# A recurrent attention kernel with a feed-forward layer: weight transfers moved to GpSimd's queue, w_out prepared in one operation, decay loads in pairs

## The chip, the cores and the metric

The kernel runs on one core of a Trainium2 chip. Its engines are TensorE (PE, matrix products), VectorE (DVE), ScalarE (ACT), GpSimd (POOL) and SyncE (SP, which here issues transfers). Each engine takes its own instructions in order and waits on semaphores for the others. The metric is the time of one execution in microseconds on the device, lower being better; a profiled execution also gives a span, from its first to its last instruction.

## The reference

The first part is a linear-attention recurrence over 768 steps for 4 batches and 8 heads of width 48. The state decays by a given factor `w` for every step and channel. The second part takes the 3072 rows of 384 numbers that come out and applies a layer of width 1024, with a softmax gate and a normalization between its two weight matrices.

```python
for t in range(S):
    kt, vt, rt, wt = (k[:, :, t], v[:, :, t], r[:, :, t], w[:, :, t])
    cur = np.einsum('bhd,bhe->bhde', u[None] * kt, vt)
    y[:, :, t] = np.einsum('bhd,bhde->bhe', rt, state + cur)
    state = wt[:, :, :, None] * state + np.einsum('bhd,bhe->bhde', kt, vt)
...
h = x @ w_in
e = np.exp(h - h_max)
sm = e / (np.sum(e, axis=-1, keepdims=True) + 1e-09)
solu = h * sm
ln = (solu - mu) / np.sqrt(var + 1e-06) * g_ln
return (ln @ w_out).astype(np.float32)
```

All inputs and the output are float32.

## The kernel before

The work is cut into 24 units, one for each of 6 chunks of 128 steps and each of the 4 batches; the batch runs fastest, so units 4 to 7 are the second chunk of batches 0 to 3. Within a chunk the recurrence becomes matrix products. For one unit the steps, with the names by which the list of the order calls them, are these:

- `ldw`, `ldk`, `ldr`, `ldv` load four tiles of 128 x 8 x 48 numbers through SP, each row of 48 numbers (192 bytes) being one piece of the transfer.
- `lw` takes the logarithm of w (ACT), `cum` sums it over time by matmuls with triangular matrices, `exp` exponentiates the sums in place (ACT), `et` and `kp` scale (DVE).
- `p`, `q`, `dg`, `dv` form the bonus with u, `qa` being a shorter way to the sum in `dg`; `vb` casts v to bfloat16.
- `kt` and `kr` transpose and copy, `M`, `m`, `sel` make the masked scores, `Y` and `y` the attention's output (with an x behind it, `Y` adds the bonus by one more matmul), `S` and `st` the new state, `X` and `xT` its transpose.
- `H` multiplies by w_in (24 matmuls), `e` exponentiates (ACT), `he` multiplies (DVE), `hq` squares, `Oa` and `Ob` multiply by the prepared w_out (`w2`) and gather sums; `sq`, `qm`, `lv`, `rs` compute the scale of a row; `o` applies it and `sto` stores.

A long text, `ORDER`, writes out the order of all these steps. Each word is a step, a unit and, where there is a choice, the engine (`a` ACT, `v` DVE, `g` POOL). The class `InOrder` ties every instruction of an engine behind the one before it on that engine, so this text is each engine's program; on the profile nearly all instructions carry the line of that class (L71). The words `dm` are matmuls on zeros whose results are not used.

Set-up that stands in the same order: `ldwin` loads w_in in three pieces of 512 KB and `ldwout` loads w_out in two of 768 KB, all through SP, as float32. `win` casts each piece of w_in to bfloat16 (ACT). `gw` scales a slice of w_out, 128 x 384, by the gain (eight slices, on ACT, POOL and DVE), `mean` multiplies all eight by a constant matrix on TensorE, `mean_sb` copies the mean, and `wt` adds it to each slice (eight additions, all on POOL), which gives `w2`. `small` loads u and the gain, `rows` and `ubc` spread them over the partitions. The constants of `make_identity` are not tied into POOL's order by `InOrder`, and stand behind `p` of unit 0 on POOL.

Of the kernel before, what the change touches and what calls it, by code (L numbers as in the profile page):

```python
# [9 lines left out]
F32 = mybir.dt.float32  # L10
# [4 lines left out]
SQUARE = mybir.ActivationFunctionType.Square  # L15
IDENTITY = mybir.ActivationFunctionType.Identity
# [8 lines left out]
dm5 dm3 dm18 dm1 ldw0 ldr0 small dm16 dm8 ldk0 lw0 ldw1 ldr1 cum0 exp0 et0 lw1 rows cum1 ldk1 p0g ldw2 kp0 exp1 ubc kt0 p1g kr0v ldr2 M0 ldk2 ldv0 et1  # L25
kp1 lw2 m0a q0g kt1 kr1v ldwin2 cum2 q1g sel0 dg0 exp2 M1 dm10 et2 vb0a kp2 m1a ldwin1 ldv1 kt2 win2a dg1 dv0g kr2v win1a vb1a Y0 y0v sel1 ldwin0 M2
win0a dm6 X0 m2v dv1v ldwout0 dm4 p2g Y1 q2g S1 y1v ldwout1 qa2 gw1a gw0a dm2 X1 xT0v xT1v dg2 H0 H1 ldw3 e0 st1 S0 dm13 ldv2 gw4v gw6v gw3g he0 ldk3
gw5a dm12 dm17 ldw4 st0 gw7a ldr3 e1 ldk4 lw3 gw2g mean mean_sb:a vb2g ldw5 dv2g he1 Y2 ldr4 cum3 wt2g y2v exp3 lw4 et3 p3v hq0a wt3g cum4 wt1g X2 dm0
wt0g ldk5 dm9 ldr5 exp4 lw5 ldw6 wt4g kp3 S2 kt3 ldv3 cum5 st2 ldw7 wt7g ldv4 et4 kr3a xT2v wt6g ldr6 Oa0 kp4 p4v exp5 wt5g M3 q3v et5 m3a kt4 kr4v
ldk6 Oa1 kp5 hq1a H2 M4 q4g kt5 Ob0 ldv5 sel3 ldw8 lw6 vb3a e2 dg3 kr5a dv3g m4v sq0a dg4 vb4g dv4g p5g vb5g Ob1 ldr7 M5 lw7 ldk7 Y3x ldv6 he2 m5v qm0  # L30
q5g p6g y3a cum6 X3 xT3v sq1v Y4 qm1 exp6 y4v H3 lv0 lv1 et6 ldr8 X4 hq2v ldk8 kp6 Oa2 dg5 o0a xT4a dv5g p7g sto0 ldw9 S4 e3 S3 st4 st3 q6g H4 Y5 vb6g
q7g ldr9 o1a he3 kt6 lw8 S5 Ob2 e4 ldk9 y5v cum7 ldr10 he4 kr6a st5 X5 hq3a sq2a exp7 M6 Oa4 ldv7 ldk10 ldr11 Oa3 qm2 m6v cum8 ldv8 qa6 et7 xT5a sto1
dg6 ldr12 ldk11 lv2 kp7 qa7 Ob3 dv6g exp8 p8g ldw10 p9v kt7 et8 o2a dg7 sq3g kp8 H5 qm3 q8g hq4a lv3 ldv9 e5 ldw11 Y6x kr7v ldv10 p10g M7 vb7g o3v Ob4
ldw12 kt8 m7v y6a q10g lw9 X6 sq4v he5 cum9 xT6a qm4 ldk12 exp9 kr8a dg8 et9 dv7g Y7 hq5g H6 e6 sto2 kp9 Oa5 ldw13 kt9 y7v lv4 X7 dg10 q9g Ob5 kr9a
he6 vb8g ldv11 ldk13 dv8g ldr13 sq5a o4a M8 ldw14 hq6g m8v S7 M9 qm5 vb10g xT7a p11g ldv12 m9v lv5 Oa6 H7 dg9 st7 lw10 Y8 o5a e7 cum10 vb9g ldw15
exp10 Ob6 y8v he7 sq6g X8 sto3 et10 dv9g S6 kp10 ldk14 xT8a lw12 S8 q11g H8 lw11 lw13 cum11 st8 e8 dv10g st6 Oa7 qm6 kt10 Y9x p12g exp11 hq7v kr10a
lv6 Ob7 y9a he8 M10 et11 S9 ldw16 sto4 o6a ldr14 X9 xT9a kp11 cum12 qa11 Oa8 ldr15 exp12 hq8g m10v p13g ldv13 vb11g ldk15 st9 H9 sq7v et12 qm7 kt11
q12g ldv14 lw14 ldr16 kp12 ldk16 lv7 e9 Y10x q13g sto5 y10a o7v ldk17 kr11v he9 cum13 exp13 ldv15 et13 dg11 kt12 kp13 Ob8 X10 sto6 M11 kr12a sq8g Oa9
qa12 ldk18 dv11g ldr17 dg13 M12 m12v kt13 ldw17 vb12g xT10a qm8 S10 m11a sel11 H10 kr13v M13 lw15 st10 ldv16 hq9a Y11x lv8 p15g e10 y11a m13v vb13g
sto7 o8a Ob9 dg12 p14g ldr18 ldv17 sq9v dv12g p16g X11 ldw18 cum14 xT11a S11 he10 Y12 H11 exp14 S12 qm9 st11 y12v lv9 et14 kp14 q14g dv13g st12 hq10g  # L40
o9a ldv18 e11 Y13 X12 cum15 xT12a ldr19 he11 exp15 kt14 Oa10 y13v sto8 hq11g kr14a vb15a q15g lw16 S13 H12 vb14g et15 ldk19 kp15 e12 dg14 X13 M14 p17g
dv14g kt15 ldw19 m14v xT13a he12 kr15a Ob10 H13 q17g sto9 hq12g sq10a st13 M15 Y14 m15v ldv19 qm10 lv10 vb16g Oa11 e13 lw18 q16g S14 lw17 o10v y14v
cum16 he13 ldw20 exp16 dg15 et16 hq13v Ob11 dv15g X14 kp16 Oa12 p18g sq11a p19g xT14a st14 qm11 lv11 H14 Ob12 o11a e14 cum17 q19g kt16 sq12v ldk20 Y15
sto10 he14 exp17 q18g qm12 Oa13 sto11 kr16a et17 hq14g y15v cum18 kp17 lv12 Ob13 M16 ldr20 ldk21 o12v exp18 dg17 X15 vb17g sq13v kt17 m16a et18 qm13
Oa14 xT15v kp18 kr17v sel16 lv13 H15 o13a lw19 dg16 e15 kt18 M17 dv17g dv16g vb19g ldv20 kr18v m17a lw20 Ob14 Y16 he15 M18 y16v sq14v S16 qm14 dg18
cum19 X16 ldv21 hq15g xT16v m18a exp19 Oa15 H16 ldw21 sel17 S15 dg19 lv14 o14a et19 kp19 Y17 lw21 ldr21 st16 e16 cum20 sel18 vb18g st15 y17v exp20
Ob15 sto12 ldk22 ldr22 X17 sto13 kt19 sq15v ldv22 xT17a he16 dv18g Y18 qm15 kr19a dv19g kp20 p20v y18v hq16g H17 M19 Oa16 lv15 X18 q20g Ob16 m19v o15a
e17 xT18a ldw22 lw22 p22g cum21 sq16v he17 qm16 p21g dg20 ldw23 hq17g ldv23 exp21 Y19 kt20 H18 vb20g ldr23 Oa17 lv16 y19v kp21 q21g kr20v o16a cum22
e18 he18 dv20g kt21 exp22 Ob17 kr21a M20 X19 sq17g S17 qm17 m20a lv17 kp22 qa21 sel20 lw23 S18 xT19v sto14 o17a st17 hq18g M21 Oa18 ldk23 m21v kt22
cum23 H19 sto15 st18 exp23 kr22v vb21a kp23 dg21 dv21g sto16 Y20 Y21 vb22a M22 q22g S19 e19 m22a vb23g y20v X20 p23v st19 he19 q23g Ob18 kt23 xT20a  # L50
sq18v H20 qm18 kr23a sel22 M23 y21v lv18 o18a X21 dg22 hq19v xT21v Oa19 m23a dv22v dg23 sel23 Y22 Ob19 y22v e20 he20 H21 dv23g Y23 sto17 X22 sq19a
Oa20 y23v X23 qm19 lv19 hq20g o19a xT22v e21 xT23v H22 e22 he21 Ob20 sto18 hq21g sq20a qm20 lv20 H23 he22 Oa21 Oa22 sto19 Ob21 e23 hq22g sq21a o20v
qm21 lv21 Ob22 he23 hq23v Oa23 sto20 sq22v sq23a qm22 o21v Ob23 sto21 lv22 qm23 Oc23 o22v sto22 lv23 dm14 oz23v dm15 o23a stz23 dm7 sto23 dm11 dm19
# [25 lines left out]
def kernel(  # L79
# [38 lines left out]
    def load(name, src):  # L118
        def stage(i):
            c, b = units[i]  # L120
            L = live[i]
            if name in "kr":

                if "k_and_r" not in L:
                    L["k_and_r"] = io.tile([C, 2, H, 64], F32, tag="kr_in", name="kr_in")
                t = L["k_and_r"][:, "kr".index(name)]
            else:
                t = io.tile([C, H, 64], F32, tag=name + "_in", name=name + "_in")
            L[name] = t[:, :, :D]
            sp.dma_start(out=L[name], in_=src[b, :, c * C:(c + 1) * C, :].rearrange("h t d -> t h d"))  # L130
        return stage
# [4 lines left out]
    win_f = consts.tile([128, KM, DF], F32)  # L136
    win_v = moe_w_in.rearrange("(ko ki) f -> ki ko f", ki=128)
    wout_f = consts.tile([128, KF, DM], F32)
# [5 lines left out]

    def load_w_in(j):
        sp.dma_start(out=win_f[:, j, :], in_=win_v[:, j, :])

    def load_w_out(half):
        part = slice(half * KF // 2, (half + 1) * KF // 2)
        sp.dma_start(out=wout_f[:, part, :], in_=wout_v[:, part, :])  # L150
# [3 lines left out]
    nc.gpsimd.memset(uti_neg, -1.0)  # L154
    nc.gpsimd.affine_select(out=uti_neg, in_=uti_neg, compare_op=ALU.is_ge, fill=0.0, base=0,
                            pattern=[[1, C]], channel_multiplier=-1)
    uts = consts.tile([C, C], BF16)
    nc.gpsimd.memset(uts, 1.0)
    nc.gpsimd.affine_select(out=uts, in_=uts, compare_op=ALU.is_gt, fill=0.0, base=0,
                            pattern=[[1, C]], channel_multiplier=-1)  # L160
    ident = consts.tile([C, C], BF16)
    make_identity(nc, ident)
# [12 lines left out]
    lw_t = [consts.tile([C, H, 64], BF16, name=f"lw{j}") for j in range(NR)]  # L175
    kp_t = [consts.tile([C, 2, H, 64], BF16, name=f"kp{j}") for j in range(NR)]
    for j in range(NR):
        nc.vector.memset(lw_t[j][:, :, D:], 0.0)
        nc.vector.memset(kp_t[j][:, :, :, D:], 0.0)
# [4 lines left out]
    win_sb = consts.tile([128, KM, DF], BF16)  # L184
    w2 = consts.tile([128, KF, DM + 1], BF16)

    mean_w = consts.tile([128, 128], BF16)
    nc.vector.memset(mean_w, -1.0 / DF)
    nc.vector.memset(w2[:, :, DM:], 1.0 / RDF)

    ident_f = consts.tile([KF, KF], F32)
    make_identity(nc, ident_f)
# [4 lines left out]
    gw = consts.tile([128, KF, DM], BF16)  # L197
# [12 lines left out]

    def copy(engine, out, in_):
        if engine is act:
            act.copy(out=out, in_=in_)
        else:
            engine.tensor_copy(out=out, in_=in_)
# [6 lines left out]
    def setup_w_in(j, engine):  # L222
        copy(engine, win_sb[:, j, :], win_f[:, j, :])


    def setup_gain(f, engine):
        if engine is act:
            act.activation(out=gw[:, f, :], in_=wout_f[:, f, :], func=COPY, scale=gr[:, f:f + 1])
        else:
            engine.tensor_scalar(out=gw[:, f, :], in0=wout_f[:, f, :], scalar1=gr[:, f:f + 1], scalar2=None, op0=MULT)  # L230

    def setup_mean():
        m_ps = small.tile([128, DM], F32, tag="s", name="mean_ps")
        for f in range(KF):
            pe.matmul(m_ps, lhsT=mean_w, rhs=gw[:, f, :], start=(f == 0), stop=(f == KF - 1))
        live[0]["mean_ps"] = m_ps

    def setup_mean_copy(engine):
        copy(engine, mean_sb, live[0]["mean_ps"])
# [400 lines left out]
```

The softmax here doesn't subtract the row's maximum and nothing guards it: scores larger than these inputs give would overflow.

## Time and profile before

| | |
|---|---|
| three runs | 157.39, 151.35 and 157.56 us, median 157.39 |
| profiled execution | 151.29 us, of which 149.6 us are its span |
| mean granted TensorE clock | 0.966 |
| busy: TensorE, DVE, ACT, POOL | 137.2, 127.0, 119.7, 122.9 us |
| transfers | 27.09 MB in 104970 packets, of which 100329 are under 512 bytes |

Busy time is the sum of an engine's instructions. A group of instructions is named by engine, operation and tiles, with a count and the mean length of one. The costliest groups are the matmuls of `O` (42.3 us for 200), those of `H` (35.9 us for 576), DVE's `he` (29.2 us for 24, 1.218 each), POOL's squares `hq` (26.5 us for 14, 1.892 each), ACT's `e` (24.5 us for 24, 1.020 each) and DVE's `kp` (22.8 us for 24, 0.948 each). Matmul lengths overlap one another, so a group's sum can exceed the time it took up. An SP row's length contains the wait for room in the transfer queue.

### The profile page before, as it was taken

The page shows a single profiled execution, that of the slowest core. Times are in us where ns is not written, and L with a number is a line of the kernel's source. Part 1 is how long each engine was busy: PE and PEld are TensorE (multiplying, and loading weights), DVE is VectorE, ACT ScalarE, POOL GpSimd, SP SyncE. Part 2 cuts the span into 40 slices and gives each one's busy share as a digit, 9 for nine tenths or more (in the row PEclk, how much of TensorE's full clock was granted, in tenths as well). Part 3 has the DMA queues.
Part 4 walks back from the last instruction along what each step waited for, and adds up shares of the span by engine and source line. Part 5 has one row for each costly group of instructions (what it writes and reads, how often), then busy time and mean ns, then how long its engine had stood idle before and what let it go on. Part 6 is the DMA issues. An engine that isn't in the chain of part 4 may idle for free.

```text
span 149.6 us, 5293 instructions
## 1 busy us (share of the span) xinstructions
PE 137.2 (92%) x2154; PEld 108.7 (73%) x2156; DVE 127.0 (85%) x231; ACT 119.7 (80%) x232; POOL 122.9 (82%) x152
## 2 busy tenths in 40 slices
PE   5676887698999999999999999999999999999993
PEld 2254584576886887887878888878787878888780
DVE  7547849999999798999989989988999999997661
ACT  3466768989798979799898998898998798895651
POOL 3366965999989799999989999999798989975900
PEclk9965599999999999999999999999999999999999
DMA  4999998999989999979999999999989211011113
GB/s 95 199 211 314 385 318 169 221 196 184 201 160 234 183 225 204 240 151 228 207 200 219 240 210 235 202 249 188 254 194 228 62 57 53 7 53 57 48 48 119
DMA packets 104970, 27.09 MB, mean 181 GB/s; under 512 B 100329, under 2 KB 104562, under 8 KB 104946
## 3 DMA queue, kind: packets, MB, share of 16 engines
q1 hardware_dynamic: 104946, 26.75, 79.2%
q8 instruction: 17, 0.28, 0.8%
q14 instruction: 7, 0.06, 0.1%
HBM read 22.03 MB, written 4.72 MB: 179 GB/s over the span
## 4 chain that ended last, share of the span: by engine, by line
PE 57%; POOL 10%; DMA 10%; DVE 8%; SPq 8%; ACT 3%; issue 3%; POOLq 0%; DVEq 0%
PE o_ps L71 20%; PE h_ps L71 16%; SPq L71 7%; DMA wout_f<-in_moe_w_out_dram 6%; POOL w L71 5%; PE kr_ps L71 4%; PE y_ps L71 4%; PE s_ps L71 3%; PE cum_ps L71 3%; PE m_ps L71 3%; DMA kr_in<-in_k_dram 3%; PE x_ps L71 2%; POOL dv L71 2%; DVE kp L71 1%; DVE he L71 1%
## 5 line engine op out<-in xcount | busy, mean ns | idle before, releaser
L71 PE MATMUL o_ps<-w,he 128*128 128x385 bf16 (+2 forms) x200 | 42.3, 315 | 0.3 <-ACT sq L71 0.3
L71 PE MATMUL h_ps<-xT,win_sb 128*128 128x128 bf16 x576 | 35.9, 219 | 0.1
L71 PEld LDWEIGHTS <-win_sb 128*128 128x128 bf16 x576 | 32.9, 98 | 0.8 <-issue 0.2
L71 DVE TENSOR_TENSOR he<-h_ps,e 128x1024 bf16<-128x1024 f32 x24 | 29.2, 1218 | 2.9 <-ACT e L71 2.8
L71 PE MATMUL o_ps<-inv_col,e 128*128 128x1 bf16 x192 | 31.1, 165 | 0.0
L71 ACT ACTIVATE e<-h_ps 128x1024 bf16<-128x1024 f32 x24 | 24.5, 1020 | 6.2 <-PE h_ps L71 6.1
L71 POOL TENSOR_TENSOR hq<-he 128x1024 bf16<-128x1024 bf16 x14 | 26.5, 1892 | 2.6 <-DVE he L71 2.1
L71 PEld LDWEIGHTS <-he 128*128 128x128 bf16 x208 | 19.7, 96 | 10.5 <-issue 0.3
L71 ACT ACTIVATE cum_ps<-cum_ps 128x772 f32<-128x772 f32 (+1 forms) x24 | 19.3, 803 | 5.3 <-PE cum_ps L71 4.1
L71 DVE TENSOR_TENSOR kp<-cum_ps,kr_in 128x768 bf16<-128x768 f32 x24 | 22.8, 948 | 0.2 <-ACT cum_ps L71 0.2
L71 POOL TENSOR_TENSOR q<-p,u_bc 128x384 bf16<-128x384 bf16 x23 | 21.2, 925 | 0.7 <-DVE p L71 0.5
L71 POOL TENSOR_TENSOR dv<-vb,dg 128x384 bf16<-128x384 bf16 x22 | 18.5, 845 | 3.0 <-ACT vb L71 1.1
L71 PEld LDWEIGHTS <-kp 128*128 128x128 bf16 x272 | 17.3, 100 | 4.4 <-DVE kp L71 2.3
L71 POOL TENSOR_TENSOR p<-kr_in 128x384 bf16<-128x384 f32 x18 | 18.4, 1025 | 2.5 <-DMA kr_in<-in_k_dram 2.4
L71 DVE TENSOR_TENSOR m<-m_ps,uts 128x1024 bf16<-128x1024 f32 x14 | 17.0, 1222 | 3.0 <-PE m_ps L71 2.9
L71 PEld LDWEIGHTS <-e 128*128 128x128 bf16 x192 | 18.3, 96 | 0.1
L71 PE MATMUL kr_ps<-ident,kp 128*128 128x128 bf16 x192 | 15.7, 228 | 1.9 <-DVE kp L71 1.9
L71 PEld LDWEIGHTS <-kr 64*128 64x128 bf16 (+1 forms) x272 | 10.7, 98 | 4.9 <-DVE kr L71 2.1
L71 ACT COPY kr<-kr_ps 128x1024 bf16<-128x1024 bf16 x13 | 13.2, 1015 | 0.6 <-PE kr_ps L71 0.6
L71 ACT ACTIVATE lw<-w_in 128x384 bf16<-128x384 f32 x23 | 11.7, 523 | 2.1 <-DMA w_in<-in_w_dram 2.1
L71 PE MATMUL m_ps<-kr 64*128 64x128 bf16 x192 | 10.2, 229 | 2.2 <-DVE kr L71 1.6
L71 POOL TENSOR_SCALAR_AFFINE_SELECT m<-m 128x1024 bf16<-128x1024 bf16 x10 | 10.9, 1100 | 1.1 <-ACT m L71 1.1
(93 smaller groups left out, 276.6 us busy)
## 6 DMA issues: line engine op xcount, KB each, us to landing
w_in<-in_w_dram SPq DMA_DIRECT2D x24, 192.0 KB, 3.8
kr_in<-in_r_dram SPq DMA_DIRECT2D x24, 192.0 KB, 3.6
kr_in<-in_k_dram SPq DMA_DIRECT2D x24, 192.0 KB, 3.9
v_in<-in_v_dram SPq DMA_DIRECT2D x24, 192.0 KB, 3.9
out_dram<-o SPq DMA_DIRECT2D x23, 192.0 KB, 3.5
win_f<-in_moe_w_in_dram SPq DMA_DIRECT2D x3, 512.0 KB, 5.4
wout_f<-in_moe_w_out_dram SPq DMA_DIRECT2D x2, 768.0 KB, 8.6
out_dram<-o SPq DMA_DIRECT2D x2, 96.0 KB, 1.6
```

The lines of the kernel that those rows point to most:

```text
L71: made = make(*args, **kwargs)
```

## The change

Five things are changed, and the order is written anew for all of them.

1. w_in and w_out are loaded by transfers that POOL issues. The transfer of w_in casts to bfloat16, and the float32 copy and the three casts on ACT are gone; w_out arrives as `float32r`, the same numbers in a type that a matmul takes. A one-element copy on POOL, which reads what a given load brought, stands before the first w_in transfer (w of unit 2) and before the first w_out transfer (piece 1 of w_in), so that POOL reaches them only after these have landed.
2. The mean is computed from w_out itself, by matmuls with the gain spread over 128 columns (`gm`, ACT), in two halves (`meanA`, `meanB`); the factor -1/1024 is put in when the mean is copied, on DVE. Four slices are scaled on ACT into `w2` and get the mean added on POOL; the other four are scaled and centred by one operation on DVE.
3. From unit 4 on, w is loaded for two units by one transfer, and one logarithm serves both.
4. The constants on POOL are made by one loop that `InOrder` ties in ahead of everything else.
5. `ORDER` also moves steps between engines. Squares: POOL 14 to 9, ACT 5 to 8, DVE 5 to 7. `kr` copies: ACT 13 to 7, DVE 11 to 17. Score copies `m`: ACT 10 to 12, DVE 14 to 12, and masks `sel` 10 to 12. `vb`: ACT 6 to 2, POOL 18 to 20, DVE 0 to 2. Output scaling `o`: ACT 17 to 20, DVE 7 to 4. Shorter sums `qa`: 6 to 9.

The tiles that loads fill keep their rows of 64 numbers of which 48 are used.

The diff without the whole order, of which the head is shown, new and old:

```diff
 ORDER = """
-dm5 dm3 dm18 dm1 ldw0 ldr0 small dm16 dm8 ldk0 lw0 ldw1 ldr1 cum0 exp0 et0 lw1 rows cum1 ldk1 p0g ldw2 kp0 exp1 ubc kt0 p1g kr0v ldr2 M0 ldk2 ldv0 et1
-kp1 lw2 m0a q0g kt1 kr1v ldwin2 cum2 q1g sel0 dg0 exp2 M1 dm10 et2 vb0a kp2 m1a ldwin1 ldv1 kt2 win2a dg1 dv0g kr2v win1a vb1a Y0 y0v sel1 ldwin0 M2
-win0a dm6 X0 m2v dv1v ldwout0 dm4 p2g Y1 q2g S1 y1v ldwout1 qa2 gw1a gw0a dm2 X1 xT0v xT1v dg2 H0 H1 ldw3 e0 st1 S0 dm13 ldv2 gw4v gw6v gw3g he0 ldk3
-gw5a dm12 dm17 ldw4 st0 gw7a ldr3 e1 ldk4 lw3 gw2g mean mean_sb:a vb2g ldw5 dv2g he1 Y2 ldr4 cum3 wt2g y2v exp3 lw4 et3 p3v hq0a wt3g cum4 wt1g X2 dm0
+ldw0 dm8 dm11 dm7 small dm14 dm0 ldk0 ldr0 p0g dm6 ldw1 ldk1 lw0 ldr1 cum0 ldw2 exp0 et0 ldk2 rows ldr2 lw1 ldv0 ldw3 kp0 ldk3 ubc kt0 q0g cum1 kr0v
+exp1 ldv1 iwin0 dm1 M0 lw2 ldr3 iwin1 dm18 et1 kp1 m0a kt1 cum2 p1v exp2 dm15 vb0a q1g kr1v dm3 et2 kp2 sel0 p2g M1 m1a sel1 vb1g dg0 kt2 kr2v iwin2
+dv0g gm:a Y0 q2v iwout0 M2 lw3 cum3 iwout1 dg1 exp3 dv1v Y1x p3v dm12 et3 dm17 y0v kp3 X0 ldv2 S0 kt3 m2v y1a kr3v X1 xT1v ldw4 ldv3 xT0a dm9 q3g qa3
+H0 dg2 vb2v e0 st0 H1 dv2g S1 he0 Y2x e1 st1 M3 hq0g y2a S2 dg3 X2 meanA gw0a m3a ldr4 xT2a meanB he1 st2 sel3 H2 gw7a dm16 gw6a hq1v mean_sb:v lw4
+cum4 vb3a ldk4 wt0g exp4 wt1v dv3g wt7g wt6g e2 gw4a wt2v dm19 wt4g wt3v ldw6 Oa1 ldr5 Y3x et4 ldk5 S3 kp4 he2 kt4 ldv4 cum5 wt5v ldr6 y3a p4v q4g
...
+            elif name == "w":
+                if i % 2 == 0:
+                    t2 = io.tile([C, 2, H, 64], F32, tag="w_in", name="w_in", bufs=4)
+                    for a in range(2):
+                        live[i + a]["w2_in"] = t2
+                        live[i + a]["w"] = t2[:, a, :, :D]
+                if i >= 4:
+                    sp.dma_start(out=L["w2_in"].rearrange("t a h d -> t (a h) d")[:, :, :D],
+                                 in_=src[b:b + 2, :, c * C:(c + 1) * C, :].rearrange("b h t d -> t (b h) d"))
+                else:
+                    sp.dma_start(out=L["w"], in_=src[b, :, c * C:(c + 1) * C, :].rearrange("h t d -> t h d"))
+                return
...
-    win_f = consts.tile([128, KM, DF], F32)
+    win_sb = consts.tile([128, KM, DF], BF16)
-    wout_f = consts.tile([128, KF, DM], F32)
+    wout_f = consts.tile([128, KF, DM], F32R)
...
+    def after(loaded):
+        n_seen.append(1)
+        pool.tensor_copy(out=seen[:, len(n_seen):len(n_seen) + 1], in_=loaded)
+
     def load_w_in(j):
-        sp.dma_start(out=win_f[:, j, :], in_=win_v[:, j, :])
+        if j == 0:
+            after(live[2]["w"][:1, 0, :1])
+        pool.dma_start(out=win_sb[:, j, :], in_=win_v[:, j, :])
 
     def load_w_out(half):
+        if half == 0:
+            after(win_sb[:1, 1, :1])
         part = slice(half * KF // 2, (half + 1) * KF // 2)
-        sp.dma_start(out=wout_f[:, part, :], in_=wout_v[:, part, :])
+        pool.dma_start(out=wout_f[:, part, :], in_=wout_v[:, part, :])
...
+    def setup_gain_wide(engine):
+        copy(engine, g_wide, gr.unsqueeze(2).to_broadcast([128, KF, 128]))
...
     def setup_gain(f, engine):
-        if engine is act:
-            act.activation(out=gw[:, f, :], in_=wout_f[:, f, :], func=COPY, scale=gr[:, f:f + 1])
-        else:
-            engine.tensor_scalar(out=gw[:, f, :], in0=wout_f[:, f, :], scalar1=gr[:, f:f + 1], scalar2=None, op0=MULT)
+        act.activation(out=w2[:, f, :DM], in_=wout_f[:, f, :].bitcast(F32), func=COPY, scale=gr[:, f:f + 1])
+        live[f]["scaled"] = True
+
+    def setup_mean(half):
...
+            pe.matmul(live[0]["mean_ps"], lhsT=g_wide[:, f, :], rhs=wout_f[:, f, :], start=(f == 0), stop=(f == KF - 1))
...
     def setup_w2(f, engine):
-        engine.tensor_add(out=w2[:, f, :DM], in0=gw[:, f, :], in1=mean_sb)
+        if "scaled" in live[f]:
+            engine.tensor_add(out=w2[:, f, :DM], in0=w2[:, f, :DM], in1=mean_sb)
+        else:
+            engine.scalar_tensor_tensor(out=w2[:, f, :DM], in0=wout_f[:, f, :].bitcast(F32), scalar=gr[:, f:f + 1], in1=mean_sb,
+                                        op0=MULT, op1=ALU.add)
...
+        if len(both) == 2:
+            act.activation(out=t.rearrange("t a h d -> t (a h) d")[:, :, :D],
+                           in_=live[i]["w2_in"].rearrange("t a h d -> t (a h) d")[:, :, :D], func=LN)
```

## The prediction

> **What bounds the kernel now.** I read the busy slices first. They say which stage still has slack, and the four engine shares of the page (92, 85, 80, 82%) cannot say that.
>
> ```profile
> PE   5676887698999999999999999999999999999993
> PEclk9965599999999999999999999999999999999999
> ```
>
> Each digit is a slice of 3.74 us. From slice 11 (about 40 us) to the last one TensorE is full at full clock, so from there the end is fixed by the matmul work still to do. What can move is the work done before 40 us. The table by stretch (engine, busy us and instructions in brackets, then clock, DMA share, GB/s) shows where that is lost.
>
> ```profile
> 7.50:10.00 2.50, 1.72 (x23) 1.14 (x22) 1.43 (x4) 1.25 (x2) 1.37 (x2) 0.65 1.06 210
> 25.00:27.50 2.50, 1.02 (x13) 0.75 (x13) 2.48 (x5) 2.21 (x5) 2.42 (x4) 1.00 1.09 218
> 27.50:30.00 2.50, 2.23 (x33) 1.58 (x30) 2.50 (x6) 2.25 (x4) 2.50 (x3) 1.00 1.12 224
> 32.50:35.00 2.50, 1.92 (x36) 1.73 (x34) 2.47 (x6) 1.68 (x4) 2.50 (x3) 1.00 0.82 163
> ```
>
> The columns are PE, PE weight loads, DVE, ACT, POOL. Between 25 and 40 us TensorE idles 1.48 + 0.27 + 0.58 + 0.25 (37.5 to 40) = 2.6 us while DVE and POOL are full. Later windows lose only 0.32 (50 to 60) and 0.24 (110 to 120) = 0.56 us. The chain of waits, in order of time (start, length), names the path through this stage.
>
> ```profile
> 13.03 9.62 DMA wout_f<-in_moe_w_out_dram
> 22.67 1.12 ACT gw L71 x2
> 23.79 0.81 ACT e L71
> 24.60 0.51 ACT lw L71
> 25.12 0.37 ACT mean_sb L71
> 25.56 7.74 POOL w L71 x8
> 33.30 0.87 POOL q L71
> ```
>
> The second half of w_out lands at 22.65 us; scaling, mean and eight additions on POOL finish w2 at 33.30, 10.65 us later, and POOL's queue carries the chain on to 44.7. The first output matmul starts at 29.56. The DMA queue is full meanwhile (share 0.99 to 1.1 from 2.5 us on), and the weights go through it at 368 to 390 GB/s between 12.5 and 20 us.
>
> **The change part by part.** The profiled execution took 151.29 us: 149.6 of span and 1.7 around it. The shown runs are 157.39, 151.35 and 157.56, so their median lies 6.1 us above it; the sum stands on 151.3.
>
> *Removed.* ACT loses three casts of w_in (3 x 1.045 = 3.1 us, at 14.65 to 19.0), waiting then for DMA in part. The separate scaled copy goes: 2 x 1.248 on POOL, 2 x 0.416 on DVE; ACT keeps four (0.607). POOL keeps four of its eight additions (4 x 1.0), so 3.7 us leave POOL in the full stretch. DVE takes the other four as one operation each: nearest rows are the scaling (0.416), state update (0.549) and DVE's p (0.559 alone, median 1.003, beside POOL); I take 0.55, bounds 0.42 to 1.0. Mean copy moves to DVE (0.55). Ten ACT logs of two units replace twenty of 0.523: the exponential of nearly that size takes 0.80, so 2.4 us less ACT over the kernel, none of it on the end since TensorE is full. The same holds for squares moved off POOL (14 to 9 of 1.892). By the new list's counts POOL sheds some 9 us of compute, ACT about 6, DVE gains under 1.
>
> *Added to TensorE.* The mean becomes eight matmuls on w_out itself with a widened gain. Bounds per matmul are 1.46/8 = 0.18 (bf16 row) and 0.455 (float32, 0.91 for two); I take 0.3. Four run before the second half lands, so 1.2 us follow it. The widened gain on ACT (128 x 1024) is about one cast, 1.0, long before its use. Identity constants move ahead of p0 on POOL; the 2.0 us wait for ident_f at 7.3 disappears, but kp0, done at 7.0, holds kt0 anyway, so about 0.3 us in a DMA-fed stage: nothing at the end.
>
> *Moved: five weight transfers to POOL's queue.* No POOL-issued transfer is in the trace. Lower bound for an issue is SP's shortest, 0.28 (g_rows), upper SP's longest, 3.79 (a k load at 18.73, its queue full); I take 1.0, near the middle of SP's rows of 0.4 to 1.8 between 9.7 and 14.1 us. The new list queues POOL as p0, q0, hold for w of unit 2, w_in 0, w_in 1, q1, mask 0, p2, mask 1, vb1, w_in 2, dv0, hold for w_in 1, two w_out, q3. Walking it: q0 ends 8.4; w2 landed at 9.55 (same eighth place in SP's queue), so the first hold costs 1.1 us of idle; two issues 11.6; q1 12.5 (it waits for DVE's p1, 11.4); mask 0 13.6; p2 14.6; mask 1 15.7; vb1 16.2; third issue 17.2; dv0 18.1; two issues 20.2. The second hold is past by then: w_in 1, issued at 11.6, needs about 3 us. Behind the holds wait q1 and the masks, and behind these y0 and y1. From issue to landing, 768 KB at 385 GB/s is 2.0 us, and win_f's shortest is 4.9 behind others. So w_in 2 lands near 20.2 (H0 19.53 before) and w_out near 24.5, 1.9 later than now; with issues of 0.28 it is 20.9, with 3.79 it is 38.
>
> The row that bears on POOL and DVE together is p on DVE: 0.559 at best and 1.825 at worst for one shape. The Trainium skill (SBUF — State Buffer, Who interferes with whom, with its box on DVE blocking DMA) speaks against the change: GpSimd writes the descriptors of its transfers, and a DVE operation holding the shared ports delays it, 620 ns becoming about 3100 in its example. By that figure five issues would cost 15 us of POOL, and w_out would land some 10 us later, a loss; by the rows above they cost 5. No run here shows a GpSimd transfer yet.
>
> *After landing.* DVE's new queue is st0, he0, st1, dg3, he1, st2, hq1, mean copy, w2 for 1, 2, 3. With H0 at 20.2 to 21.6 and the exponential 1.02, he0 ends 23.9, then 0.8, he1 (1.22) 25.9, st2 26.5, hq1 (0.81) 27.3, mean 27.8 and three w2 29.5. The mean matmuls end at 25.7 and are covered by this up to a landing near 26.6. So the first output starts at 29.5, as now, but TensorE has by then done H2 (1.36) and M3 (0.33) more and cum5 (0.40) less: 1.3 us ahead. POOL adds w2 0 to 28.8, dv3 29.6, w2 7, 6, 4 to 32.6, q4 33.5, against 34.17 for q4 before with mask 3 and dv3 (1.1 + 0.83) still to come: 2.6 us ahead. Since the chain between 25.56 and 44.7 runs through POOL, I take POOL's lead rather than TensorE's, and the later idle 0.56: 3.2 us.
>
> **Sum.** 151.3 - 3.2 = 148.1 us. With TensorE's lead alone it is 149.4; with TensorE's lead and all its later idle (1.3 + 2.6 + 0.56) gained, 146.8.
>
> **Rivals.** *Cheap issue.* At 0.28 each w_out lands near 21; DVE still sets the first output, but POOL leads 3.5 us more in the stretch that is full. TensorE then gains the whole 4.5 us of the last bound and two fillers fewer (0.4): 146.4. For it: SP's shortest rows. Against: DVE is full from 25 us.
>
> *No net effect.* The two w_in transfers issued first (1 MB, 2.7 us at 385 GB/s) run ahead of v0 on the shared DMA engines. Mask 1 waits for m1 on ACT, queued behind vb0, which waits for v0 (landed 12.98); mask 1 then ends near 17.6 instead of 15.7, and third issue, H0 and landing move with it by 1.9. Left are 3.2 - 1.9 = 1.3, less what w2 costs on DVE beside POOL (4 x 0.45 at the 1.0 bound) as far as POOL's lead doesn't cover it: about 150.5. For it: the DMA share is 1.0 there. The Trainium skill (DMA: Bandwidth & Descriptors, Queues, rings and completion order) has each DMA engine alternate between queues packet by packet, so long weight rows would get more than half beside the 192-byte rows of a load, which speaks for this case; in the trace all data shares one queue, and no row can show it. A weaker form of the case: the holds hold nothing, as POOL reaches the first about when w2 lands.
>
> *Slower: the issues hold POOL.* If one issue costs c us of POOL, three of them lie before H0 and five before w_out has landed: H0 moves by 3(c - 1) and the landing by 5(c - 1), of which DVE covers 2.1 (24.5 to 26.6). The end moves by the larger of 3(c - 1) and 5(c - 1) - 2.1. At c = 1.9, POOL's longest compute instruction, that is 2.7 and the time 150.8; the gain is gone at c = 2.06; from c = 2.65 on the kernel is slower by over 2%; at c = 3.0 the time is 148.1 + 7.9 = 156.0, and at SP's longest, 3.79, it is 160. For it: 128 rows and more must be described for each transfer, and SP, which does little else, already needs up to 3.79. Against: SP's long rows are waits for a full queue, and POOL's would be another queue.
>
> **How the numbers follow.** Forecast 0.51, cheap issue 0.15, no net effect 0.10, slower 0.24. From 151.3, 2% is 3.0 us, about what measuring this kernel can tell from no change: faster means under 148.3. Cheap issue and two thirds of the forecast's own range (146.8 to 149.4; 0.58 of it lies under 148.3, and what POOL and ACT shed later is counted at nothing) give 0.15 + 0.34 = 0.49, rounded to 0.50; the rest of the forecast and no net effect give 0.17 + 0.10, with rounding 0.26; slower 0.24. The range 145.5 to 155.5 cuts some 0.04 at the bottom and 0.14 at the top, issues above 2.9 us, which no POOL instruction of the trace comes near.
>
> **What would show it.** Right: POOL issues near 1 us; w_out landed before 26.6; w2 finished at 32 to 33; first output near 29.5 with H2 before it; TensorE nearly full from 27.5 on. Wrong: POOL idle at a hold, v0 landing after 14, or H0 after 22. A low clock reaching into 20 to 30 us, where 10 us of matmuls would double, would upset the sum from outside it: it now lies at 8 to 18.5 us (0.65, 0.50, 0.50, 0.50, 0.80), mostly beneath DMA waits.

## The result, and the profile after

| | before | after |
|---|---|---|
| ratio of undisturbed runs | 1 | 1.0145, interval 1.0092 to 1.0198 |
| profiled execution | 151.29 us | 155.1 us |
| its span | 149.6 us | 153.4 us |
| first output matmul | 29.56 us | 34.45 us |

The kernel became slower by 1.45%; 148.1 us was predicted, with 145.5 to 155.5 as the range. The medians of all runs (155.53 before, 154.91 after) point the other way only because many runs of before were disturbed; the ratio leaves such runs out.

The busy slices of the changed kernel, 3.84 us each:

```profile
PE   6884368787999999999999999999999999999991
PEclk9999758999999999999999999999999999999999
```

From slice 11 on TensorE is full at full clock, as before. So the loss lies before 40 us again. The table by stretch (busy time and instructions of TensorE, weight loads, DVE, ACT and POOL, then clock, DMA share, GB/s) says how much; the first two lines are of the changed kernel, the next two of the kernel before.

```profile
0.00:20.00 20.00, 12.16 (x92) 6.47 (x94) 11.12 (x44) 9.74 (x13) 10.02 (x23) 0.93 0.88 166
20.00:40.00 20.00, 16.65 (x212) 12.67 (x212) 18.15 (x29) 12.56 (x19) 14.56 (x17) 0.90 1.11 238
```

```profile
0.00:20.00 20.00, 13.60 (x113) 8.21 (x115) 13.48 (x49) 11.13 (x14) 11.35 (x23) 0.74 0.93 250
20.00:40.00 20.00, 17.22 (x258) 13.41 (x257) 17.73 (x31) 17.39 (x32) 17.87 (x21) 1.00 1.01 205
```

In 40 us TensorE was busy 12.16 + 16.65 = 28.8 us instead of 30.8, with 304 matmuls instead of 371. The 2.0 us, and 1.3 us by which its whole busy time grew (138.5 against 137.2), are 3.3 of the 3.8 us. Two windows of the changed kernel place most of the idle time.

```profile
15.00:17.50 2.50, 0.40 (x8) 0.32 (x9) 1.07 (x3) 0.05 (x1) 0.39 (x1) 0.91 1.17 226
17.50:20.00 2.50, 0.88 (x6) 0.49 (x6) 0.39 (x1) 1.32 (x2) 0.92 (x2) 0.50 0.64 127
```

From 15 to 20 us no engine does much: TensorE idles 3.7 of 5 us. The clock is 0.50 from 17.5 to 22.5 us and 0.72 in the 2.5 us behind that, so the low clock that the prediction named as a danger for 20 to 30 us did come in part; H0 and H1 still took 2.84 us, as before. The chain of waits names what all wait for (start, length; rows of "issue" under 0.1 us are left out):

```profile
11.79 7.24 DMA v_in<-in_v_dram
19.08 0.50 POOL vb L72
19.58 0.54 POOL win_sb L72
20.14 0.84 POOL dv L72
20.98 0.47 POOL seen L72
21.45 0.76 POOL wout_f L72
22.21 9.17 DMA wout_f<-in_moe_w_out_dram
31.42 0.97 PE mean_ps L72 x4
```

v of unit 1 needs 7.24 us from its issue to its landing, and the second half of w_out 9.17; before, w_out had landed at 22.65. The third piece of w_in is not on this chain but came just as late: issued at 19.53, it landed at 24.91, level with the start of H0 at 24.90, whose third matmul needs it. POOL's timeline shows what stood behind v1 (idle time before an instruction, and what ended it, in square brackets):

```profile
10.00 0.18 POOL L72 COPY seen<-w_in 1x1 f32<-1x1 f32 x1 [1.40 <-DMA w_in<-in_w_dram]
10.13 1.29 POOL L72 DMA_DIRECT2D win_sb<-in_moe_w_in_dram  x2
...
14.30 1.09 POOL L72 TENSOR_SCALAR_AFFINE_SELECT m<-m 128x1024 bf16<-128x1024 bf16 x1
19.08 0.50 POOL L72 CAST vb<-v_in 128x384 bf16<-128x384 f32 x1 [3.69 <-DMA v_in<-in_v_dram]
19.53 0.59 POOL L72 DMA_DIRECT2D win_sb<-in_moe_w_in_dram  x1
...
21.39 1.57 POOL L72 DMA_DIRECT2D wout_f<-in_moe_w_out_dram  x2
```

An issue costs POOL 0.55 to 0.82 us. The holds are cheap too. But the third piece of w_in and both halves of w_out stand behind the cast of v1, where POOL idles 3.69 us. The DMA view in stretches of 2 us (queue, packets, MB, share of the engines) shows why v1 is late: q1 holds SP's loads, q0 POOL's transfers. First 8 to 10 us, then 14 to 16 us:

```profile
q1 hardware_dynamic: 2181, 0.41, 104.7%
```

```profile
q0 software_dynamic: 162, 0.30, 81.7%
q1 hardware_dynamic: 569, 0.11, 30.0%
```

Alone, SP's queue moves 2181 packets of 192 bytes in 2 us; beside two pieces of w_in, a quarter of that (583 in the 2 us before).

### The profile page after: what moved, and what is told of

It reads as the page before. It is cut to its first block, busy times and chain, and to the rows that moved or that the text cites. A ratio compares the mean times of both kernels' runs of the same rounds, so it can differ in the third digit from the quotient of the medians.

```text
span 153.4 us, 5277 instructions
## 1 busy us (share of the span) xinstructions
PE 138.5 (90%) x2156; PEld 109.2 (71%) x2157; DVE 127.8 (83%) x236; ACT 115.5 (75%) x218; POOL 118.2 (77%) x157
## 4 chain that ended last, share of the span: by engine, by line
PE 64%; DMA 14%; SPq 7%; DVE 5%; ACT 3%; issue 2%; POOL 2%; ACTq 0%
PE o_ps L72 22%; PE h_ps L72 17%; SPq L72 6%; DMA wout_f<-in_moe_w_out_dram 6%; PE kr_ps L72 5%; DMA v_in<-in_v_dram 5%; PE y_ps L72 4%; PE cum_ps L72 4%; PE m_ps L72 4%; DMA out_dram<-o 4%; PE s_ps L72 3%; PE x_ps L72 2%; DVE w L72 1%; DVE kp L72 1%; ACT e L72 1%
## 5 line engine op out<-in xcount | busy, mean ns | idle before, releaser
L72 ACT ACTIVATE e<-h_ps 128x1024 bf16<-128x1024 f32 x24 | 24.5, 1022 | 8.0 <-PE h_ps L72 7.6
L72 PEld LDWEIGHTS <-he 128*128 128x128 bf16 x208 | 19.6, 96 | 10.1
L72 POOL TENSOR_TENSOR q<-p,u_bc 128x384 bf16<-128x384 bf16 x23 | 21.7, 944 | 1.6 <-DVE p L72 1.0
L72 POOL TENSOR_TENSOR hq<-he 128x1024 bf16<-128x1024 bf16 x9 | 17.0, 1890 | 7.5 <-DVE he L72 7.3
L72 POOL TENSOR_TENSOR p<-kr_in 128x384 bf16<-128x384 f32 x20 | 19.9, 1001 | 3.5 <-DMA kr_in<-in_r_dram 3.5
L72 POOL TENSOR_TENSOR dv<-vb,dg 128x384 bf16<-128x384 bf16 x23 | 19.3, 841 | 2.2 <-DVE dg L72 1.5
L72 DVE TENSOR_TENSOR m<-m_ps,uts 128x1024 bf16<-128x1024 f32 x12 | 14.6, 1216 | 0.7 <-PE m_ps L72 0.4
L72 POOL TENSOR_SCALAR_AFFINE_SELECT m<-m 128x1024 bf16<-128x1024 bf16 x12 | 13.5, 1128 | 1.1 <-ACT m L72 0.9
L72 POOL CAST vb<-v_in 128x384 bf16<-128x384 f32 x20 | 10.2, 508 | 5.4 <-DMA v_in<-in_v_dram 3.7
L72 DVE COPY kr<-kr_ps 128x1024 bf16<-128x1024 bf16 x17 | 11.7, 686 | 2.5 <-PE kr_ps L72 2.5
L72 ACT ACTIVATE lw<-w_in 128x768 bf16<-128x768 f32 (+1 forms) x13 | 10.0, 766 | 4.7 <-DMA w_in<-in_w_dram 4.7
```

Source lines behind the costliest of these rows:

```text
L72: made = make(*args, **kwargs)
```

## The experiments

Each ratio stands against the kernel before, run on the same chip in the same set. The theory first formed was this (A): *the weights and the loads are now two queues on the same DMA engines, so whichever is early makes the other late; v1, and behind it H0 and w_out, pay.* Against it stood the price of POOL's issues and holds (B), and the new way of preparing w2, above all on DVE (C).

**v1 first** (e1). `ldw3 kp0 ldk3` give way in SP's list:

```diff
-ldv0 ldw3 kp0 ldk3 ubc kt0 q0g cum1 kr0v exp1 ldv1
+ldv0 ldv1 ldw3 kp0 ldk3 ubc kt0 q0g cum1 kr0v exp1
```

> The changed kernel with one load moved: v of unit 1 goes third from where it stood, ahead of w and k of unit 3. Theory A (the weight transfers on POOL's queue take the DMA engines from the loads; v1 lands at 19.05 us, vb1 on POOL waits for it and holds the third w_in transfer and both w_out transfers behind it): v1, issued near 10.1, lands near 15 to 16, the third w_in transfer is issued near 16 to 17 instead of 19.53, H0 starts near 21.5 to 22.5 instead of 24.9, and the kernel is 1.5 to 3 us faster than the changed one (152 to 153 beside 154.5). Theory B (a POOL-issued transfer is slow in itself, whatever waits ahead of it): issue moves but H0 and the time do not. Theory C (the new order of the rest is what costs): under 0.5 us either way.

1.0179 (1.0084 to 1.0274), so not the gain of 1.5 to 3 us that A gave. v1 was cast at 17.04 instead of 19.08, w_out issued from 19.00 instead of 21.4 and landed at 28.6 instead of 31.4, and nobody waited for it. Yet H0 began at 23.89, only 1.0 earlier, since DVE had unit 3's p ahead of the last transpose for H0, and that waited 1.25 us for r3. The first output came at 33.97, 10.1 us after H0. H0 and H1 also ran at a lower clock (0.50 and 0.62 in the windows from 22.5 to 27.5 us) and took 4.29 us for the 48 matmuls that the changed kernel does in 2.84:

```profile
23.89 4.29 PE L80 MATMUL h_ps<-xT,win_sb 128*128 128x128 bf16 x48
```

So they ended at 28.18, later than in the changed kernel (27.74), and the earlier start bought nothing. In this list the chain of waits runs from unit 3's loads through its steps on DVE to H0, and from there through DVE to the mean and w2; in the changed kernel w_out's landing and this chain arrive together (DVE free at 32.29, the mean's matmuls done at 32.39). By its time alone e1 fits B and C as well as A. What it shows is that w_out landing 2.8 us earlier is not enough.

**Hold on v1** (e2): the first hold reads v1 instead of w of unit 2.

```diff
-            after(live[2]["w"][:1, 0, :1])
+            after(live[1]["v"][:1, 0, :1])
```

> The changed kernel with the first hold reading v of unit 1 instead of w of unit 2, so that no weight is asked for until the loads up to v1 have landed. Theory A: without weights beside it v1 lands about 3.6 us after its issue, near 15.5; the two first w_in transfers go out then and the third right after q1, masks, p2 and vb1, near 20; H0 moves to about 25 to 26, so the time stays within 1 us of the changed kernel: loads gain what weights lose. Theory B predicts that v1 lands at 19 as before, since the weights would not be what delays it. Theory C: no difference in time.

1.0375 (1.0296 to 1.0453). With the weights held, v1 landed at 15.50, 3.5 us earlier; this is the other side of A. w_in was issued at 15.6, H0 came at 27.37 and the first output 9.3 us behind it at 36.70.

**No holds** (e3): both one-element copies taken out.

> The changed kernel without the two one-element copies, so that POOL issues the first w_in transfers right after q0 (8.6 us instead of 10.13) and w_out without waiting. Theory A: the holds themselves cost little (1.4 us of idle POOL, 0.5 for the second); starting weights 1.4 us earlier crowds w2, k2, r2 and v0 as well as v1, and vb1 still holds the third w_in: time within 1 us of the changed kernel, v1 landing no earlier than 18. Theory D (the holds are the loss): H0 2 us earlier and the time 2 us lower.

1.019 (1.0122 to 1.0258), w_in issued at 8.34, w_out landed at 30.1, H0 at 24.78, first output at 34.42, 9.6 us behind. The holds have no effect that shows beside the 1.0145 of the change.

**New w2 alone** (e4): the kernel before with w_out through POOL at 12.4 us, the mean from w_out, and slices 2, 3, 4 and 6 in one operation on DVE; w_in stays on SP.

> The kernel before with one part of the change: w_out through POOL, issued where SP issued it (near 12.5 us, no hold), the mean taken from w_out itself, and w2 for slices 2, 3, 4, 6 in one DVE operation; w_in stays on SP with its casts, order otherwise as before. If the w2 part is what the change gains: w_out lands within 1 us of 22.65, w2 is finished about 3 us before 33.3, and the kernel is 0.5 to 2 us faster than before. If a POOL-issued w_out is slow in itself (theory B), it lands after 25 and the kernel is slower than before by 2 us or more.

1.0267 (1.0208 to 1.0326). H0 at 19.52, as before, and w_out landed at 24.05, 1.4 late; but the first output came at 33.57, 4.0 late. POOL waited 5.30 us for v2, DVE's pieces came at 27 to 33 us ahead of its p and kp, and POOL waited 4.5 us for those. This is no test of C by itself: w_out in a second queue stretched v2, which landed 11.6 us after its issue, and the two losses are mixed. No run has the new w2 with w_out left on SP.

**Weights ahead** (e5), then the same on 64-byte bounds (e9), and without SP's hold (e6). POOL issues all five transfers between its steps, SP holds unit 3's loads by a small transfer that reads w_out, and unit 3's steps move behind H1:

```diff
+    held = consts.tile([1, 1], F32)
+    def hold_sp():
+        sp.dma_start(out=held, in_=wout_f[:1, 0, :1].bitcast(F32))
...
-        if half == 0:
-            after(win_sb[:1, 1, :1])
```

> The changed kernel with the order of arrival of the kernel before: POOL issues all five weight transfers between the bonus steps from about 10 us on, and SP holds the loads of unit 3 and later back until the first half of w_out has landed; the steps of unit 3 stand behind the second H in the order. Nothing is left out. Theory A (the weights came late because loads of units 3 to 5 shared the DMA engines with them): w_out landed at 21 to 24 us instead of 31.4, H0 at 19.5 to 21 instead of 24.9, first output at or before 30.5, time 148 to 151.5. Theory B (the price of POOL's issues and of two queues, whatever the order): w_out landed after 26, time 153 to 155. Theory C (the pieces of w2 on DVE set the first output, not the arrival): w_out early as in A, first output still at 33 or later, time 153 to 155.

> As the run with the weights ahead, but SP holds nothing back: the loads of units 3 and 4 keep the places in SP's list that the change gave them. All else equal. Theory A (sharing): w_out is issued by about 14 us and yet lands only at 26 to 30, since unit 3's four loads, v2, v3 and the pair of w (1.6 MB, 7 to 8 us at 210 to 224 GB/s) share the engines with it; time 152 to 155. Theory B (only the late issue mattered): w_out lands 21 to 24, time as in the run with the hold, within 0.7 us of it.

1.0838 (1.0763 to 1.0913) with SP's hold, 1.0558 (1.0491 to 1.0626) without. w_out landed at 24.7 and 23.8 us, but the time did not follow: v1, though ahead of unit 3's loads in SP's list and issued about when the first weights were, was now later than ever. POOL in e6:

```profile
21.28 0.50 POOL L80 CAST vb<-v_in 128x384 bf16<-128x384 f32 x1 [4.22 <-DMA v_in<-in_v_dram]
```

H0 began at 25.88, and unit 3's steps behind it then held the mean and the first output. A's numbers were missed, because they let the weights move early for nothing: the price is paid by v1. e5 was worse than that. Its `held` tile of 4 bytes had moved the load tiles 32 bytes off 64-byte bounds:

> The run with the weights ahead once more, with one difference: the small tile that SP's hold writes is 256 bytes long instead of 4, so that the load tiles behind it start on multiples of 64 bytes again, as in the kernels before and after; with 4 bytes they started 32 bytes off. If the start of the load tiles matters: loads alone move 0.40 to 0.45 MB in 2 us instead of 0.33, time 153 to 159. If it does not: 163.5 to 166, as in that run, and the cause of its loss is elsewhere.

1.0579 (1.0469 to 1.0689) with a tile of 256 bytes, 160.59 us instead of 164.86. That is a little above the 153 to 159 expected if the start of the load tiles matters, and below the 163.5 to 166 expected if it does not. The same on the kernel before (e10), with one unused tile of 4 bytes:

```diff
+    shift = consts.tile([1, 1], F32)
     u_row = consts.tile([1, DM], F32)
```

> The kernel before with one unused tile of 4 bytes ahead of all others, which moves the load tiles 32 bytes off 64-byte bounds; nothing else. If the start of the load tiles matters: the loads of the first 35 us go at 162 GB/s instead of 205 to 215, a load takes 1.2 us instead of 0.9, some 20 loads are 6 us later, time 156 to 163. If it does not: 151.2 to 152.5.

1.091 (1.0809 to 1.101); the median of 165.02 us is above the 156 to 163 expected. The DMA view from 6 to 10 us, before and then off bounds:

```profile
q1 hardware_dynamic: 4391, 0.83, 105.2%
```

```profile
q1 hardware_dynamic: 3468, 0.65, 152.8%
```

A fifth fewer packets of the same 192 bytes land in the same time. The tile moves all tiles behind it by 32 bytes, not those of the loads alone. e5 is thus no evidence on the weights; e6 and e9 are.

**Late weights** (e7): the kernel before, all on SP, six loads moved ahead of weights in SP's list; v1, too, now stands ahead of two pieces of w_in.

```diff
-ldv0 ... ldwin2 ldwin1 ldv1 ldwin0 ldwout0 ldwout1 ldw3 ldv2 ldk3 ldw4 ldr3 ... ldv3
+ldv0 ldw3 ldk3 ldv1 ldr3 ldwin2 ldwin1 ldwin0 ldv2 ldw4 ldv3 ldwout0 ldwout1
```

> The kernel before, all weights still on SP, with six loads in SP's list moved ahead of weights: w, k and r of unit 3 ahead of w_in, and v2, w4 and v3 also ahead of w_out. Nothing else is touched. Theory A (order of arrival alone): each load of 197 KB takes 0.9 us at 218 GB/s, so H0 moves by some 2.7 us to 22.2 and w_out's landing by 5.4 to 28.1; the first output moves by 4 to 5.4 to 33.5 to 35; time 153.5 to 156.5, as slow as the changed kernel or slower, with no transfer on POOL at all. Theory B (POOL's transfers or DVE's pieces cause the loss): time 151 to 152.5.

1.0393 (1.0337 to 1.0448), without a transfer on POOL. H0 began at 22.46 (22.2 expected) and w_out's two transfers landed 5.8 and 7.1 us after issues at 20.6 and 21.3, so at 28.4 (28.1 expected); the first output came at 35.35. Here the chain of waits does run from w_out's landing. Late weights alone, in one queue, cost more than the change.

**w unit by unit** (e8): the changed kernel without the pairs.

> The changed kernel with w loaded and its logarithm taken unit by unit again, the second of a pair right behind the first on SP and on ACT. Nothing is left out. If the pairs are free, as the prediction had it (2.1 to 2.4 us of ACT, none on the end): within 0.6 us of the changed kernel, 154.2 to 155.6. If the double transfer of w (393 KB at once) is part of the loss: 152 to 153.5. If the saved ACT time counted: 156 to 157.5.

1.0182 (1.0119 to 1.0244), 154.45 us against 154.91 for the changed kernel in another set. The pairs neither cost nor give anything that shows.

**Weights kept from v1, a new list** (e11), and **unit 3 later** (e12). e11 puts y0 ahead of dv1 and dv0 ahead of vb1, holds SP until the last piece of w_in has landed, and unit 3's steps stand behind H0; e12 is e1 with unit 3's steps behind H0.

> The changed kernel's work with a list that keeps the weights and v1 apart: v0 and v1 are the last loads ahead of the weights, SP holds the loads of units 3 and later until the last piece of w_in has landed, POOL issues all five weight transfers by about 14 us, dv0 stands ahead of vb1 on POOL and y0 ahead of dv1 on DVE, and the steps of unit 3 stand behind H0 and H1 (p3 on POOL, the copy kr3 on ACT). Nothing is left out. Theory A (arrival order and the in-order waits behind it make the loss): v1 landed by 15.5, H0 at 19.5 to 21, w_out landed by 23.5, first output by 31.5, time 149 to 152. Theory B (something in the new way of preparing w2 costs as much even with early data, DVE's pieces above all): w_out landed by 24, first output after 33, time 153 to 155.

> The run with v1 first, with unit 3's steps (log, sums, p, kp, their transposes, q) moved behind the last x copy ahead of H0 on every engine; SP's and POOL's lists unchanged. Nothing is left out. If H0 is late because unit 3's loads and 3.4 us of its DVE steps stand ahead of it (p3 alone waits 1.25 us for r3 there): H0 at 20.5 to 22 instead of 23.9, first output 31.5 to 33, time 152 to 153.5. If the landing of w_out near 31 sets the first output by itself: H0 early, the mean still ends at 31.5 or later, first output 33.5 to 34.5, time 154 to 155.

e11: 1.041 (1.0292 to 1.0528). w_out landed at 22.7 and v1 was cast at 19.35; H0 began at 22.61, ran at half clock (48 matmuls in 4.21 us instead of 2.84), and the first output came at 38.14. In the list of e11 DVE's pieces waited for dg3, and cum4 for a log behind m3. Neither theory's numbers were met. e12 settled nothing: H0's first matmuls came at 20.70 and the rest at 22.10, as expected, but kp3 made DVE wait 4.93 us with st0 and he0 behind it, and its lowest time was 156.03 against 150.55 for the lowest of before.

**The queue alone** (e13, e14). Every run so far that moved a weight to another queue changed the list as well. Here the kernel before keeps its code and its list but for five words: the float32 weight transfers are issued by POOL in e13 and by ACT in e14.

```diff
-        sp.dma_start(out=win_f[:, j, :], in_=win_v[:, j, :])
+        pool.dma_start(out=win_f[:, j, :], in_=win_v[:, j, :])
...
-        sp.dma_start(out=wout_f[:, part, :], in_=wout_v[:, part, :])
+        pool.dma_start(out=wout_f[:, part, :], in_=wout_v[:, part, :])
```

> The kernel before with its five weight transfers (float32, same pieces, no cast) issued by POOL instead of SP: two pieces of w_in behind q0, the third behind q1, both halves of w_out behind mask 0, so at about 10.5 to 14 us, as SP issues them now (9.7 to 14.1). The loads keep SP's list, now without the weights in it. Nothing else changes. Theory A (two queues share the engines and stretch each other, small loads most): v1 and the loads of unit 3 advance at a quarter to a third of their rate while the weights run; H0 or the unit 3 steps 1.5 us or more later, time 152.5 to 157. Theory B (only the changed kernel's own list and late issue cost time): H0 within 0.7 us of 19.5, w_out landed at 21.5 to 24, time 150.5 to 152.

> The same with ACT in POOL's place: the five weight transfers are issued by ACT behind lw2, m0 and exp2 (about 10 to 14 us). If a second queue is what costs: as with POOL, within 1 us of that run. If GpSimd's way of making transfers costs: ACT's run stays at 150.5 to 152 and POOL's does not.

e13: 1.0145 (1.008 to 1.0211). On the kernel before, this edit alone costs as much as the whole change does. Its timeline of TensorE, H0 with H1:

```profile
20.98 4.47 PE L80 MATMUL h_ps<-xT,win_sb 128*128 128x128 bf16 x48
```

and its DMA view from 18 to 20 us, followed by that of the kernel before:

```profile
q0 software_dynamic: 167, 0.73, 88.2%
q1 hardware_dynamic: 426, 0.08, 19.9%
```

```profile
q1 hardware_dynamic: 530, 0.79, 106.6%
```

The engines move 0.81 MB in the one case and 0.79 in the other. The second queue brings no rate; it only lets unit 3's loads, which stood behind the weights in SP's one queue, run beside them. They take a fifth of the engines' time for a tenth of the bytes, and are themselves stretched: the slowest loads take 11.8 to 12.4 us from issue to landing, against 5.1 to 6.2 before. H0 comes 1.45 us later, H0 and H1 take longer (4.47 against 2.84 us for the same 48 matmuls, at a clock of 0.78 and then 0.54), and the first output, at 32.15, is 2.6 us late.

The way there is not that of the changed kernel. v1 landed at 13.28, in time; it was the second piece of w_in that came late beside the loads (17.33, before 15.92), and ACT's list has its cast ahead of that of v1 (start, length, from the chain of waits):

```profile
17.35 1.04 ACT win_sb L80
18.39 0.42 ACT vb L80
```

The cast of v1 began at 18.30 in place of 16.89, and through dv1, y and the transposes H0 went with it. This is the other side of the sharing, weights late beside loads. Of the 3.1 us by which H1 ends later, 1.6 are the lower clock; why it was lower was not tested. Nor was the opposite edit: no run has the changed kernel with its five transfers back on SP.

e14: 1.0535 (1.0462 to 1.0609), and no test of what it was meant for. ACT's two issues of w_out took 0.40 and 0.46 us, but the second began 3.2 us after the first had ended; ACT did nothing in between, and the casts of v0 and m1 stood behind it until 21 us. What a second queue of the other kind would cost without that stays open.

**Two additions on DVE** (e15): `wt5` and `wt6` of the kernel before from POOL to DVE.

> The kernel before with two of POOL's eight additions of the mean (slices 5 and 6) on DVE, behind kp3 and st2; both operands are bfloat16. POOL sheds 2.0 us in the stretch from 25.6 to 33.3 that the chain of waits runs through, DVE takes 0.35 to 0.56 each if it is like its other bfloat16 products. If POOL's chain sets the idle 2.6 us of TensorE between 25 and 40 us: 0.5 to 1.5 us faster, 149.7 to 151. If DVE, as full there, is the bound: 151 to 152.5.

1.0031 (1.0005 to 1.0056). On DVE they took 1.06 and 0.60 us; the first output moved from 29.56 to 30.08. No run here beat the kernel before, and none pointed to a list that would.

## Why the prediction was wrong

*Right.* That only the work before 40 us could move. The issue price: 1.0 taken, 0.55 to 0.82 measured. The Trainium skill (SBUF — State Buffer, A bandwidth-pool intuition that's wrong (but worth ruling out)) has a GpSimd transfer go from about 620 to about 3100 ns beside a `tensor_copy` on DVE; POOL's issues at 21.4 take 0.79 each with DVE busy throughout. But DVE was then not copying from SBUF to SBUF, here or beside an issue of any other run, so its example was not put to the test. POOL's walk up to mask 1 (15.7 predicted, 15.39 measured), the first hold (9.55 against 10.0), the second hold without a wait. The widened gain (1.0; 1.05). The walk behind H0 came out by luck: 7.9 to 9.3 us from H0 to the first output by the prediction's own numbers, 9.55 measured. Its condition was three pieces of w2 done on DVE. These were done only 11.0 us after H0, at 35.92, as one took 0.97 there and not 0.55; the first output began earlier because it took the slice that POOL had ready at 34.40, and the fourth output matmul then waited 0.78 us for DVE.

*The step that failed: POOL's walk at "vb1 16.2", and with it "H0 at 20.2 to 21.6".* The cast of v1 was given only the time of POOL's queue, as if v1 landed as before. It began at 19.08. The loads were left their old speed while 1 MB of w_in ran in a second queue; measured, they kept a quarter of it. Third issue (17.2 predicted; 19.53), dv0 and w_out's issues moved with it. H0 came at 24.90. Two things that this step had earlier end together there: the third piece of w_in, put "near 20.2" by the prediction, landed at 24.91; and behind dv1 DVE had to do all this ahead of H0:

```profile
20.14 1.27 DVE L72 TENSOR_TENSOR p<-kr_in 128x384 bf16<-128x384 f32 x1
21.33 0.15 DVE L72 TENSOR_TENSOR et<-cum_ps,own 128x8 f32<-128x8 f32 x1
21.41 0.54 DVE L72 TENSOR_TENSOR y<-y_ps,dv 128x384 bf16<-128x384 f32 x1
21.87 0.94 DVE L72 TENSOR_TENSOR kp<-cum_ps,kr_in 128x768 bf16<-128x768 f32 x1
22.73 1.21 DVE L72 TENSOR_TENSOR m<-m_ps,uts 128x1024 bf16<-128x1024 f32 x1
23.94 0.69 DVE L72 COPY kr<-kr_ps 128x1024 bf16<-128x1024 bf16 x1
24.55 0.34 DVE L72 COPY xT<-x_ps 128x384 bf16<-128x384 bf16 x1
```

p, et, kp and kr here are unit 3's; the new list puts them ahead of the last transpose that H0 needs, and e1 shows p waiting 1.25 us for r3. So in the changed kernel neither DVE's list nor the weights alone held H0. Of the signs that the prediction named, POOL idled at a hold (1.40 us) and H0 came after 22; v0, landed at 12.57, was in time.

*The second failed term: "768 KB at 385 GB/s is 2.0 us".* That rate was read off weights that had the one queue to themselves. Beside the loads w_out took 9.2 us from its last issue, and landed at 31.4 instead of 24.5, of which 2.0 us are the later issue (22.21 against 20.2); over all runs with w_out on POOL a half took 6.2 to 10.7 us, issued anywhere from 12 to 24 us. In the kernel before the halves had taken 7.6 and 9.6 us behind others in the one queue, so 2.0 us was a rate and not a time to landing. In the changed kernel TensorE waits 1.06 us for it, with DVE done at about the same time; in e1, where it landed 2.8 us earlier, the time was the same within the intervals, with H0 and H1 at a lower clock. How the loss divides between the two terms is not shown.

*Sizes.* One operation of w2 on DVE took 0.94 (0.55 taken, bounds 0.42 to 1.0), a mean matmul 0.24 (0.3 taken). The group on DVE, shortest, median and longest in ns:

```profile
L72 DVE SCALAR_TENSOR_TENSOR w<-wout_f,gr,mean_sb x4: 625/937/1268, 33.0 to 37.9; 128x384 bf16<-128x384 f32 x4
```

Where POOL had nothing to do beside them, in e11, three took 1.67 us together, 0.56 each.

*The rivals.* The slower one named POOL's issues, and its price was not there. The one without net effect had the mechanism, weights running ahead of loads on shared engines, with the rule of the Trainium skill behind it (DMA: Bandwidth & Descriptors, Queues, rings and completion order) that each DMA engine takes its queues in turn, packet by packet. The rows agree with it in direction: 0.30 MB of weights against 0.11 of loads from 14 to 16 us, 0.73 against 0.08 in e13. But it was priced on v0 alone, at 1.9 us; v0 was in time (cast at 12.69), and v1, w3, k3 and r3 were not looked at. It should have ended on the slower side.

*Shown and not shown.* That moving the five transfers to POOL's queue makes the kernel before slower by as much as was measured for the change is shown by e13; that late weights in one queue can cost more, by e7; that v1 and the weights are late in turn, by e2, e6, e9 and e13. That v1's lateness holds the third piece of w_in, w_out and H0 in the changed kernel is read off its chain of waits and off e1, where all of them came earlier with v1; that the time would follow is not shown, since no run with an earlier v1 was faster. The change's loss is likely divided between the queue and the new list with its pieces of w2 on DVE, but no run separates the two: e13 and the change cost the same in different lists and by different paths.

## What to carry to other kernels

Where the DMA engines were full, a second queue added no bandwidth (0.81 against 0.79 MB in 2 us) and gave up the order that one queue keeps. Before moving transfers off a full queue, list every load that stands behind them in it, and every load that will now run beside them; price each of them at a share of the rate (here a quarter for the loads), and follow each to the in-order engine that waits for it. And give every small tile a size that leaves the load tiles behind it on 64-byte bounds; an offset of 32 bytes is the only other one measured here.

## What had not been expected of the hardware

- A load of 192-byte rows into tiles that start 32 bytes off a 64-byte bound is slower by a fifth (3468 packets against 4391 in 4 us), and a kernel whose start is bound by such loads by 9.1% (e10).
- POOL issues a transfer of 768 KB in 0.75 to 0.95 us and a third of w_in (256 KB as bfloat16) in 0.55 to 0.75; no packet of the two transfers issued at 10.13 moves before 12 us.
- Transfers issued on POOL overtake a load that SP issued at the same time or shortly before: v1, issued at 9.46, 9.60 and 9.86, landed 11.76, 11.21 and 9.43 us later in e6, e9 and e11, where the first weights were issued at 9.7 to 9.8; loads of v took 4.3 to 5.6 before.
- On ACT, the two issues of w_out stood 3.2 us apart and ACT did nothing between them (e14); on POOL, in the same kernel, both were done in 1.55 us (e13).
